# Hedgehog linear attention and a sigmoid GLU on one core: k tiles every six steps, a first h tile in a nest, q tasks, numerators and weight loads in other places

## The chip, the cores and the metric

One core of a Trainium2 chip. The metric is the device time of one execution in microseconds (us); given are the median, the lowest and the highest of three runs, and one further execution that was profiled. The engines are TensorE (PE, matmuls and transposes), VectorE (DVE), ScalarE (ACT), GpSimd (POOL) and SyncE (SP), which issues all the large transfers of this kernel in one queue, in order.

## The reference

x is 2048 rows (tokens) by 1024, all in fp32. It is normalised, then feeds two branches that are multiplied:

```python
def _A_ref(x, wqkv, w_phi, wo):           # H = 32 heads of 32
    q, k, v = split heads of x @ wqkv
    pq = jnp.einsum("bhsd,hdf->bhsf", q, w_phi)
    pk = jnp.einsum("bhsd,hdf->bhsf", k, w_phi)
    phi_q = jnp.concatenate([_softmax(pq, axis=-1), _softmax(-pq, axis=-1)], axis=-1)
    phi_k = jnp.concatenate([_softmax(pk, axis=-1), _softmax(-pk, axis=-1)], axis=-1)
    kv = jnp.einsum("bhsf,bhsd->bhfd", phi_k, v)
    z  = jnp.einsum("bhsf->bhf", phi_k)
    num = jnp.einsum("bhqf,bhfd->bhqd", phi_q, kv)
    den = jnp.einsum("bhqf,bhf->bhq", phi_q, z)[..., None] + 1e-6
    o = num / den
    return o (heads joined) @ wo

def _B_ref(x, w_gate, w_up, w_down):      # F = 3584
    g = jnp.einsum("bsd,df->bsf", x, w_gate)
    u = jnp.einsum("bsd,df->bsf", x, w_up)
    h = _sigmoid(g) * u
    return jnp.einsum("bsf,fd->bsd", h, w_down)

xn = _layernorm(x, axis=-1)
return x + _A_ref(xn, ...) * _silu(_B_ref(xn, ...))
```

## The kernel before

**Products.** An fp32 value is held as two reduced-precision parts: the rounded value (a cast on ACT, L135) and what is left (a subtraction on DVE, L136; "the low half" below). `mm3` (L144 to L146) is one fp32 product from three matmuls, high × high, high × low and low × high. The large products use a seven-product scheme: instead of eight products of quarter matrices there are seven, named B11, B21, T2, T3, T4, T1 and B22, of sums and differences of quarters. Weight sums are made by POOL and ACT (L483 to L485 for the GLU), stored or kept in SBUF, and then split into `w` tiles by `prep`, eight slots ahead at most.

**Stages.** First the projections of q, k and v, with the head transform `w_phi` folded into the weights of q and k, for one half of the rows, then the GLU's first pass; the projections for the other half; the second pass, pass 1 in the code (`begin_pass(1)`, L1476), which makes products T2, T3 and T4 for 14 tiles f of the hidden width; pass 2, which makes T1 and B22; then the down projection; and last an output loop over 8 pairs of row tiles, whose order is the list `PAIR`.

In pass 1 an f takes three groups of four banks. One bank is 12 matmuls, and after each comes a tick: so 12 ticks for an f, 168 for the pass. In the group T4 the gate of banks 0 and 1 is a sigmoid (L1429), banks 2 and 3 are multiplied onto it by DVE (`h_direct`, L1431), and ACT then copies the partial sum of the next f from memory into the bank (`seed`, L1392), so that T2 of the next f can accumulate there. PE waits for that copy.

In pass 2 most f are a `nest` (L1536): T1 and B22 of neighbouring tiles together, where the B22 product of a tile is itself made by seven smaller products, with its own operands (`x_nest_load`, `x_nest_sums`, `x_nest_split`). A nest has 90 matmuls and six ticks. In it ACT copies one partial result into the bank of the next product; L1612 is the copy from bank c to bank a, which product T4 accumulates onto. Before, pass 2 begins with plain T1 of tile 0, plain B22 of tile 0 and plain T1 of tile 1, and then come nests 1 to 12.

**Side work.** Everything that isn't the main product is queued by `later(n, f, ...)`: f is issued at the n-th tick from now. `k_steps` does one tile of 128 rows of k and v: load, maxima and minima per head (L663, L664), differences (L673, L674), one exponential (L677), sums and inverses (L682), scaling (L719), the low part (L727), and eight matmuls of the kv product (L735). Twelve of the 32 tiles are done during the projections, 20 in pass 1. `k_end` sums up a half of the heads. `q_steps` does the same features for a tile of q; four of these tasks run in pass 2, and they load from `qkv_d` at L951. `k_steps` tells the tiles of the projections from those of pass 1 by `wide`.

The order of instructions in one engine is set by this text order and by the scheduler of the framework, which moves instructions inside an engine by its own timeline; stretches marked `in_order` stay as they are written. An engine works its instructions strictly in order, so one that waits holds all those behind it.

Of the kernel before, what the change touches and what calls it, by code (L numbers as in the profile page):

```python
# [21 lines left out]
TT = S // P  # L22
# [27 lines left out]
def hedgehog_glu_kernel(  # L50
# [63 lines left out]
    LEAD = 2  # L114
    BEHIND = 'DVE', 'Activation', 'SP'
# [304 lines left out]
    ops += [("glu", 2, 0, T1), ("glu", 2, 0, B22), ("glu", 2, 1, T1)]  # L420
    ops += [("nest", 2, f, B22) for f in range(1, NJ - 1)] + [("glu", 2, NJ - 1, B22)]
# [17 lines left out]
    entry = {0: ops.index(("glu", 0, 0, B11)), 2: ops.index(("glu", 2, 1, T1))}  # L439
# [1021 lines left out]
    def begin_pass(p):  # L1461
# [14 lines left out]
        elif p == 1:  # L1476
            gates_r.items = halves(45, 46)
            gates_r.n = 0
            for n, f, *a in ((165, x_nest_load, 2, 0, 0), (166, x_nest_load, 2, 0, 1), (166, x_nest_load, 2, 1, 0),
                             (171, x_nest_load, 2, 1, 1), (170, x_nest_sums, 2, 0), (175, x_nest_sums, 2, 1),  # L1480
                             (176, x_nest_split, 2, T2), (177, x_nest_split, 2, T3), (179, x_nest_split, 2, T4)):
                later(n, f, *a)
            at = 1
            for t in range(EARLY, 2 * TT):
                k_steps(int(at), *divmod(t, TT))
                at += 7
                if t % TT == TT - 1:
                    k_end(int(at) + 8, t // TT)
                    at += 16
        else:  # L1490
# [3 lines left out]
            for n in range(4):  # L1494
                q_steps(13 + 18 * n, 6 + n // 2, n % 2)
# [3 lines left out]
    nest_raw = {0: ((43, 44), (54, 44)), 2: ((47, 50), (51, 53))}  # L1499
# [16 lines left out]
    def x_nest_split(p, i, hs=(0, 1)):  # L1516

        if i == T4:
# [7 lines left out]
        if i == T1 and p:  # L1526
            uvfree.extend(halves(47, 51))
# [110 lines left out]
    for n, (kind, c, what, i) in enumerate(ops):  # L1638
# [76 lines left out]
        if (phase, i) == (2, T1):  # L1715
            fetch_sum(2, f + 1)
            if f == 0:
                fetch_sum(1, 1)
# [41 lines left out]
        elif phase == 1 and f == NJ - 1:  # L1760
# [5 lines left out]
            else:  # L1766
                for b in (3, 5):
                    block(f"x{b}", 4 * b, 4, F32)
                uvfree.extend(halves(12, 13, 14, 15, 20, 21, 22, 23, 45, 46))
# [6 lines left out]
        elif (phase, f, i) == (2, 1, T1):  # L1776
# [111 lines left out]
    for k in range(4):  # L1888
        wo_prep(B22, k)
# [17 lines left out]
    for n in range(2):  # L1907
# [7 lines left out]
        gB110 mT4- xT4h- gB111 vB22- xT4l- gB112 mT1- tr100 gB113 hi100 lo100 tr001 gT20 hi001 aT1- lo001 tr000 gT21  # L1915
# [138 lines left out]
```

## Time and profile before

| what | us |
|---|---|
| median of three runs | 2344.85 |
| lowest, highest | 2343.36, 2347.31 |
| the profiled execution | 2340.34 |
| its span, first to last instruction | 2338.5 |
| PE busy | 2325.4 (99%) |
| DVE, ACT, POOL busy | 1687.9, 1252.6, 1120.4 |

The profile is of one execution. Times in its rows count from the start of its span. A row of the timeline reads: start, duration, engine, line, operation, output and inputs by name with shape and type, and in brackets how long the engine stood idle just before and what ended that; a matmul's duration there is from its issue to its end, and they overlap. A row of a group reads: line, engine, operation, count, then busy us, the mean of one in ns, and idle time ahead of it. The bound engine is PE, so the view of its waits is the one to begin with.

### The profile page before, as it was taken

To read this page: it belongs to the slowest core of one execution; us is meant where nothing else is said; L and a number is where in the kernel's file an instruction comes from. 1 tells how busy PE (TensorE), PEld (TensorE's weight loads), DVE (VectorE), ACT (ScalarE), POOL (GpSimd) and SP (SyncE) were. 2 spreads that over 40 slices of the span, in tenths; PEclk is the share of its full clock that TensorE was granted. 3 is DMA by queue.
4 is the path that set the end of the run, shared out by engine and by line. 5 is a ranking of instruction groups with operands and counts; after the bars stand their busy time and mean duration, and the time that the engine had idled before them with its cause. 6 is when DMAs were issued, how large, how long until landed. Compare 5 with 4: busy or idle time off the path is not lost.

```text
span 2338.5 us, 32642 instructions
## 1 busy us (share of the span) xinstructions
PE 2325.4 (99%) x10822; PEld 1939.5 (83%) x10822; DVE 1687.9 (72%) x2143; ACT 1252.6 (54%) x2000; POOL 1120.4 (48%) x797
## 2 busy tenths in 40 slices
PE   9999999999999999999999999999999999999999
PEld 8888888888888888888888888878888888888887
DVE  8624767776888765668656766674899878877786
ACT  7354577766555555555555555553444444355553
POOL 0323436781141055656541776674665444424566
PEclk9999999999999999999999999999999999999999
DMA  8799987988879777888795976779877667785665
GB/s 299 260 311 361 338 294 274 352 315 302 277 262 302 265 256 259 314 304 286 263 321 178 325 236 221 254 271 358 288 256 265 225 208 248 251 283 203 206 204 180
DMA packets 305018, 635.68 MB, mean 272 GB/s; under 512 B 38609, under 2 KB 38865, under 8 KB 300241
## 3 DMA queue, kind: packets, MB, share of 16 engines
q1 hardware_dynamic: 304848, 633.60, 78.5%
q8 instruction: 84, 1.38, 0.2%
q14 instruction: 86, 0.70, 0.1%
HBM read 380.50 MB, written 252.97 MB: 271 GB/s over the span
## 4 chain that ended last, share of the span: by engine, by line
PE 95%; DMA 1%; DVE 1%; ACT 1%; POOL 1%; issue 1%; SPq 0%; POOLq 0%; DVEq 0%; ACTq 0%
PE bank L144 30%; PE bank L146 30%; PE bank L145 30%; PE bank L1076 1%; PE bank L735 1%; PE bank L1052 1%; PE bank L379 1%; PE bank L1326 0%; DMA wf_d<-p 0%; PE bank L247 0%; DMA fc<-e_d 0%; DMA wd_d<-fb 0%; DMA fc<-qkv_d 0%; DMA fb<-w_gu 0%; DMA wd_d<-fa 0%
## 5 line engine op out<-in xcount | busy, mean ns | idle before, releaser
L144 PE MATMUL bank<-x,w 128*128 128x512 f32 x2252 | 877.1, 390 | 2.5 <-ACT bank L1392 2.2
L145 PE MATMUL bank<-x,w 128*128 128x512 f32 x2252 | 877.0, 389 | 0.0
L146 PE MATMUL bank<-x,w 128*128 128x512 f32 x2252 | 875.9, 389 | 0.0
L136 DVE TENSOR_TENSOR w<-fa,w 128x512 fp32r<-128x512 f32 (+2 forms) x388 | 378.4, 981 | 324.2 <-ACT w L135 315.8
L144 PEld LDWEIGHTS bank<-x,w 128*128 128x128 f32 x2252 | 423.1, 188 | 91.2 <-ACT bank L1392 3.1
L146 PEld LDWEIGHTS bank<-x,w 128*128 128x128 f32 x2252 | 422.9, 188 | 87.7
L145 PEld LDWEIGHTS bank<-x,w 128*128 128x128 f32 x2252 | 423.1, 188 | 87.1
L135 ACT CAST w<-fa 128x512 fp32r<-128x512 f32 (+2 forms) x388 | 265.1, 685 | 333.7 <-PE bank L145 233.9
L144 PE MATMUL bank<-w,x 128*128 128x512 f32 x708 | 277.5, 392 | 0.0
L146 PE MATMUL bank<-w,x 128*128 128x512 f32 x708 | 276.0, 390 | 0.0
L145 PE MATMUL bank<-w,x 128*128 128x512 f32 x708 | 276.0, 390 | 0.0
L136 DVE TENSOR_TENSOR w<-fb,w 128x512 fp32r<-128x512 f32 (+1 forms) x120 | 113.1, 947 | 67.6 <-ACT w L135 67.4
L146 PEld LDWEIGHTS bank<-w,x 128*128 128x128 f32 x708 | 133.0, 188 | 27.9 <-DVE x L1252 0.3
L144 PEld LDWEIGHTS bank<-w,x 128*128 128x128 f32 x708 | 133.0, 188 | 26.3 <-ACT bank L635 0.2
L145 PEld LDWEIGHTS bank<-w,x 128*128 128x128 f32 x708 | 133.1, 188 | 26.2
L135 ACT CAST w<-fb 128x512 fp32r<-128x512 f32 (+1 forms) x120 | 72.9, 609 | 115.4 <-PE bank L145 81.7
L136 DVE TENSOR_TENSOR x<-fb,x 128x512 fp32r<-128x512 f32 (+1 forms) x83 | 91.4, 1104 | 20.8 <-ACT x L135 19.8
L1396 ACT COPY fc<-bank 128x512 f32<-128x512 f32 x116 | 66.7, 584 | 42.5 <-PE bank L146 20.6
L136 DVE TENSOR_TENSOR p<-fc,p 128x512 fp32r<-128x512 f32 (+1 forms) x68 | 53.2, 793 | 33.3 <-ACT p L135 32.7
L1090 POOL TENSOR_TENSOR fc<-fc 128x512 f32<-128x512 f32 x32 | 48.9, 1527 | 59.2 <-DVE fc L1085 23.9
L135 ACT CAST x<-fb 128x512 fp32r<-128x512 f32 (+1 forms) x83 | 63.0, 761 | 10.9 <-DMA fb<-xo_d 5.6
L310 POOL TENSOR_TENSOR fb<-fb 128x512 f32<-128x512 f32 x6 | 9.9, 1648 | 112.9 <-DMA fb<-w_gu 76.1
(403 smaller groups left out, 3851.7 us busy)
## 6 DMA issues: line engine op xcount, KB each, us to landing
m_d<-fc SPq DMA_DIRECT2D x168, 256.0 KB, 4.2
fa<-h_d SPq DMA_DIRECT2D x147, 256.0 KB, 4.3
x<-m_d SPq DMA_DIRECT2D x130, 256.0 KB, 4.8
fa<-wf_d SPq DMA_DIRECT2D x32, 1024.0 KB, 6.6
fa<-w_gu SPq DMA_DIRECT2D x102, 256.0 KB, 5.0
h_d<-fc SPq DMA_DIRECT2D x96, 256.0 KB, 5.2
fc<-e_d SPq DMA_DIRECT2D x48, 512.0 KB, 5.8
fc<-qkv_d SPq DMA_DIRECT2D x88, 256.0 KB, 5.3
```

Of the source, the lines that this page charges most:

```text
L135: nc.scalar.copy(o[0], src)
L136: i = nc.vector.tensor_sub(o[1], src, o[0].bitcast(F32))
L144: nc.tensor.matmul(o, a[0], b[0], start=first, stop=False, **kw)
L145: nc.tensor.matmul(o, a[0], b[1], start=False, stop=False, **kw)
L146: last_mm[:] = [nc.tensor.matmul(o, a[1], b[0], start=False, stop=last, **kw).ins]
L310: nc.gpsimd.tensor_add(a22, a21, a22)
L379: nc.tensor.matmul(ps[:, gs], r[:, gs], bd[:, 4 * f + g], start=g == 0, stop=g == 3, skip_group_check=True)
L735: nc.tensor.matmul(kvb[g // 2][:, g % 2 * 256:g % 2 * 256 + 256], v[:, g].rearrange("p a f -> p (a f)"), ph[:, g].rearrange("p a f -> p (a ...
L1052: nc.tensor.transpose(ps[:, j * P:(j + 1) * P], e[:, k * P:(k + 1) * P], ident)
L1076: nc.tensor.matmul(ps[:, j * 256:(j + 1) * 256], kg[:, k], ph[:, a, k], start=a == 0, stop=a == 1)
L1090: nc.gpsimd.tensor_sub(o, a, b)
L1396: nc.scalar.copy(o, banks[b])
```

## The change

Four parts, in one edit:

1. In pass 1 a k tile starts every six ticks from tick 0 (`KAT`), where it was every seven from tick 1; its exponential, inverses, scaling and low part come one tick earlier than they did there. The x operands of pass 2's nests are loaded and split at ticks 152 to 169, where it was 165 to 179.
2. Pass 2 begins with plain T1 of tile 0 alone, and nests 0 to 12 follow.
3. The q tasks of pass 2 start at tick 7 (`CQ`) and every 18 from there, where it was 13, in a pass whose nests begin eight ticks earlier: so two ticks later in the nest that carries them. Those are the 2nd, 5th, 8th and 11th nest in both.
4. In `PAIR`, products (`gB..`, `gT..`) stand ahead of numerators (`nm...`), transposes and copies that they followed, and the preparation of weights B22 is written into the first pair (`w0` to `w3`), where it stood ahead of the loop.

```diff
+    KAT, CQ = 0, 7
...
-    ops += [("glu", 2, 0, T1), ("glu", 2, 0, B22), ("glu", 2, 1, T1)]
-    ops += [("nest", 2, f, B22) for f in range(1, NJ - 1)] + [("glu", 2, NJ - 1, B22)]
+    ops += [("glu", 2, 0, T1)] + [("nest", 2, f, B22) for f in range(NJ - 1)] + [("glu", 2, NJ - 1, B22)]
...
-    entry = {0: ops.index(("glu", 0, 0, B11)), 2: ops.index(("glu", 2, 1, T1))}
+    entry = {0: ops.index(("glu", 0, 0, B11)), 2: ops.index(("glu", 2, 0, T1))}
...
-        for n, f in ((0, k_load), (4, k_extremes), (5, k_spread), (7 + wide, lambda *a: exponentials(e_k)),
-                     (9 + wide, k_inverses), (10 + wide, k_scale), (11 + wide, k_low), (13 + 2 * wide + (t < TT - 1), kv_products)):
-            later(at + n, f, hb, t)
+        for n, f in ((0, k_load), (4, k_extremes), (5, k_spread), (7, lambda *a: exponentials(e_k)),
+                     (9, k_inverses), (10, k_scale), (11, k_low), (13 + (1 + wide) * (t < TT - 1), kv_products)):
+            later(max(at + n, 1), f, hb, t)
...
-            for n, f, *a in ((165, x_nest_load, 2, 0, 0), (166, x_nest_load, 2, 0, 1), (166, x_nest_load, 2, 1, 0),
-                             (171, x_nest_load, 2, 1, 1), (170, x_nest_sums, 2, 0), (175, x_nest_sums, 2, 1),
-                             (176, x_nest_split, 2, T2), (177, x_nest_split, 2, T3), (179, x_nest_split, 2, T4)):
+            for n, f, *a in ((152, x_nest_load, 2, 0, 0), (153, x_nest_load, 2, 0, 1), (154, x_nest_load, 2, 1, 0),
+                             (159, x_nest_load, 2, 1, 1), (158, x_nest_sums, 2, 0), (163, x_nest_sums, 2, 1),
+                             (164, x_nest_split, 2, T4, (0,)), (165, x_nest_split, 2, T4, (1,)), (166, x_nest_split, 2, T2), (169, x_nest_split, 2, T3)):
                 later(n, f, *a)
-            at = 1
+            at = KAT
             for t in range(EARLY, 2 * TT):
-                k_steps(int(at), *divmod(t, TT))
-                at += 7
+                k_steps(at, *divmod(t, TT))
+                at += 6
                 if t % TT == TT - 1:
-                    k_end(int(at) + 8, t // TT)
-                    at += 16
+                    k_end(at + 7, t // TT)
+                    at += 18
...
-                q_steps(13 + 18 * n, 6 + n // 2, n % 2)
+                q_steps(CQ + 18 * n, 6 + n // 2, n % 2)
...
-    for k in range(4):
-        wo_prep(B22, k)
...
-        hi000 e01 aT4- vB11 lo000 tr101 gT22 e11 hi101 lB22- nm001 lo101 lB21- nm000 cp001 yT1- gT23 yT4- cp000
-        ad001 gB210 ad000 nm011 vT2 gB211 cp011 ad011 tr010 gB212 hi010 lo010 gB213 mB22- tr110 nm010 hi110 aB22-
+        hi000 e01 aT4- vB11 lo000 gT22 tr101 e11 hi101 lB22- gT23 lo101 lB21- gB210 nm001 cp001 yT1- nm000 yT4- cp000
+        ad001 gB211 vT2 ad000 gB212 nm011 cp011 ad011 tr010 gB213 hi010 lo010 mB22- tr110 w0 w1 nm010 hi110 aB22- gT30
...
+        (r"w(\d)", False, lambda p, k: p or wo_prep(B22, int(k))),
```

Buffers follow (`nest_raw[2]`, the free halves of block 47 and 51, the fetch of a second partial sum that the first plain tiles needed). Most lines after the first added one stand one number higher in the changed kernel (L135 becomes L136), those near the end two lower (L1802 becomes L1800).

**The end of f = 9 in pass 1, on ACT.** T4 of f = 9 sets banks 0 to 3 (`bank_101` to `bank_104`) free for the seeds of f = 10; `w_94<-fa_97` is the cast of a later weight, `p` and `fc` belong to a k tile. Before:

```order
L1396 COPY fc_100<-bank_104 128x512
L1429 ACT_TABLE_LOAD
L1429 ACTIVATE fb_99<-bank_101 128x512
L1392 COPY bank_101<-x_3_6196 128x512
L135 CAST w_94<-fa_97 128x512
L1429 ACTIVATE fb_99<-bank_102 128x512
L1392 COPY bank_102<-x_3_6196 128x512
L135 CAST p_1_4483<-fc_100 128x8x64
L1392 COPY bank_103<-x_3_6196 128x512
L720 CAST p_4482<-fc_100 128x8x128
L135 CAST w_94<-fa_97 128x512
L1392 COPY bank_104<-x_3_6196 128x512
```

And in the changed kernel:

```order
L1429 ACTIVATE fb_99<-bank_102 128x512
L1392 COPY bank_102<-x_3_6196 128x512
L720 CAST p_4482<-fc_100 128x8x128
L1392 COPY bank_103<-x_3_6196 128x512
L1392 COPY bank_104<-x_3_6196 128x512
L136 CAST w_94<-fa_97 128x512
L1396 COPY fc_100<-bank_101 128x512
L677 ACT_TABLE_LOAD
```

The last seed, of `bank_104`, has moved from behind the weight's cast to ahead of it.

**The last nest with a q task, on DVE and ACT.** `fc_100` and `stq` belong to the q task, `w_94` are weights, `bank_105` and `bank_107` the nest's banks a and c. DVE before:

```order
L1437 TENSOR_TENSOR fc_100<-fc_100,bank_104 128x512
L136 TENSOR_TENSOR w_94<-fa_97,w_94 128x512
L663 TENSOR_REDUCE stq_11642<-fc_100 128x16
L664 TENSOR_REDUCE stq_11642<-fc_100 128x16
L1437 TENSOR_TENSOR fb_99<-fb_99,bank_101 128x512
L673 TENSOR_TENSOR fc_100<-fc_100,stq_11642 128x16x32
L674 TENSOR_TENSOR fc_100<-stq_11642,fc_100 128x16x32
L136 TENSOR_TENSOR w_94<-fa_97,w_94 128x512
L1570 TENSOR_TENSOR x_3_9768<-x_3_9768,bank_105 128x512
```

DVE in the changed kernel:

```order
L1437 TENSOR_TENSOR x_3_9819<-x_3_9819,bank_101 128x512
L137 TENSOR_TENSOR w_94<-fa_97,w_94 128x512
L663 TENSOR_REDUCE stq_11551<-fc_100 128x16
L664 TENSOR_REDUCE stq_11551<-fc_100 128x16
L1570 TENSOR_TENSOR x_3_9819<-x_3_9819,bank_105 128x512
L137 TENSOR_TENSOR w_94<-fa_97,w_94 128x512
L137 TENSOR_TENSOR w_94<-fa_97,w_94 128x256
L673 TENSOR_TENSOR fc_100<-fc_100,stq_11551 128x16x32
L674 TENSOR_TENSOR fc_100<-stq_11551,fc_100 128x16x32
```

The reductions now come after the add of the nest's first plain group, and the differences after the last two low halves. ACT before:

```order
L677 ACT_TABLE_LOAD
L677 ACTIVATE fc_100<-fc_100 128x1024
L1579 COPY p_2_10023<-bank_108 128x512
L135 CAST w_94<-fa_97 128x512
L1571 COPY bank_101<-bank_105 128x512
L1575 ACT_TABLE_LOAD
L1575 ACTIVATE x_3_9768<-x_3_9768 128x512
L135 CAST w_94<-fa_97 128x256
L1612 COPY bank_105<-bank_107 128x512
```

ACT in the changed kernel:

```order
L1579 COPY p_2_9738<-bank_108 128x512
L136 CAST w_94<-fa_97 128x512
L136 CAST w_94<-fa_97 128x256
L1571 COPY bank_101<-bank_105 128x512
L1575 ACTIVATE x_3_9819<-x_3_9819 128x512
L677 ACT_TABLE_LOAD
L677 ACTIVATE fc_100<-fc_100 128x1024
L1612 COPY bank_105<-bank_107 128x512
L1439 ACT_TABLE_LOAD
```

The exponential (L677) has moved from ahead of the nest's other work to directly ahead of L1612.

**The start of the output loop, on SP.** `g_d` takes results of the down projection, `e_d` and `wo_d` are loads for the loop. Before:

```order
L1802 DMA g_d<-x_5_12056 128x512 x2
L1904 DMA fc_100<-g_d 128x512
L1802 DMA g_d<-x_5_12056 128x512
L1042 DMA fc_100<-e_d 128x1024
L1802 DMA g_d<-x_5_12056 128x512
L1042 DMA fc_100<-e_d 128x1024
L1037 DMA x_6_16216<-wo_d 128x1024 x4
```

And in the changed kernel:

```order
L1800 DMA g_d<-x_5_12069 128x512 x2
L1900 DMA fc_100<-g_d 128x512
L1800 DMA g_d<-x_5_12069 128x512 x2
L1042 DMA fc_100<-e_d 128x1024 x2
L1037 DMA x_6_16229<-wo_d 128x1024 x4
```

Both stores now stand ahead of both `e_d` loads; the loads of `wo_d` follow as before.

More of the change, by code (lines that the diff above doesn't have):

```diff
@@ L1516, in x_nest_split @@
     def x_nest_split(p, i, hs=(0, 1)):
-        if i == T4:
+        if i == T4 and 0 in hs:
             block("p", 36, 2, F32R)
@@ L1526, in x_nest_split @@
         if i == T1 and p:
-            uvfree.extend(halves(47, 51))
+            uvfree.extend(halves(47))
             hs_r.items = halves(48, 49) + [slots[50][:, 0]]
@@ L1716, in hedgehog_glu_kernel @@
             fetch_sum(2, f + 1)
-            if f == 0:
-                fetch_sum(1, 1)
         finish()
@@ L1775, in hedgehog_glu_kernel @@
                 fetch_sum(1, 0)
-        elif (phase, f, i) == (2, 1, T1):
+        elif (phase, f, i) == (2, 0, T1):
             x_nest_split(2, T1)
```

10 lines of the change are left out of this document (5 added, 5 removed).

## The prediction

> **What bounds the kernel now.** The page first: the profiled execution took 2340.34 us, of which the span is 2338.5 us, so 1.84 us lie around it.
>
> ```profile
> span 2338.5 us, 32642 instructions
> PE 2325.4 (99%) x10822; PEld 1939.5 (83%) x10822; DVE 1687.9 (72%) x2143; ACT 1252.6 (54%) x2000; POOL 1120.4 (48%) x797
> ```
>
> TensorE (PE) is busy 99% of the span. Nothing can be won but matmuls left out or gaps between them. The view of waits (engine, line, what it waited for: total us, times, longest) lists the gaps:
>
> ```profile
> PE bank L144 <- ACT bank L1612: 2.7, 1, 2.7
> PE bank L144 <- ACT bank L1392: 2.2, 2, 1.7
> PE bank L1326 <- POOL ident masks.py:199: 1.5, 1, 1.5
> PE bank L1052 <- DMA fc<-e_d: 1.2, 1, 1.2
> ...
> PE bank L144 <- ACT bank L1600: 0.2, 1, 0.2
> ```
>
> About 8 us in all. 1.5 us of it is the start, which the change doesn't touch. So the change can win 2.7 + 2.2 + 1.2 + 0.2 = 6.3 us of gaps, what the clock lost behind them, and the removed matmuls. What it can lose is new gaps, because every other engine's work that it moves stands ahead of some copy that PE waits for.
>
> **(a) Six matmuls fewer.** The nests' side of the change replaces two plain products and one nest by other nests: an h tile of four plain groups and its partner are 2 × 48 matmuls, a nest 90, so one more nest is 96 − 90 = 6 fewer. A matmul's step comes from the chain: eight kv products end each stretch of 84 matmuls.
>
> ```profile
> 1020.60 0.95 PE bank L735 x8
> 1040.62 0.95 PE bank L735 x8
> ```
>
> (1040.62 − 1020.60 − 0.95) / 84 = 0.227 us; six are **−1.36 us**. They stand on the path with certainty, so no bounds are needed.
>
> **(b) k tiles every six ticks.** A tick is 12 matmuls, 2.72 us. Before, a k tile came every 7 ticks while an h tile takes 12, so the tile's work slid past the h tile's own side work, and twice it landed badly:
>
> ```profile
> 1157.42 0.62 ACT L135 CAST w<-fa 128x512 fp32r<-128x512 f32 x1 [4.65 <-POOL fa L484]
> 1157.95 0.58 ACT L1392 COPY bank<-x 128x512 f32<-128x512 f32 x1
> 1158.59 0.50 PE L144 MATMUL bank<-x,w 128*128 128x512 f32 x1 [0.57 <-ACT bank L1392]
> 1192.68 1.21 DVE L719 TENSOR_TENSOR fc<-fc,stk 128x1024 f32<-128x1024 f32 x1
> 1193.81 0.67 DVE L1431 TENSOR_TENSOR fb<-fb,bank 128x512 f32<-128x512 f32 x1
> 1194.52 0.59 ACT L1392 COPY bank<-x 128x512 f32<-128x512 f32 x1 [4.96 <-DVE fb L1431]
> 1195.16 0.50 PE L144 MATMUL bank<-x,w 128*128 128x512 f32 x1 [1.68 <-ACT bank L1392]
> ```
>
> In the first, the copy that seeds bank 3 (L1392) stands on ACT behind the cast of a later weight, and the cast waited 4.65 us for POOL's sum. In the second, the gate product on DVE (L1431), after which the bank may be seeded, stands behind the k tile's scaling (L719). Two tiles in twelve ticks fix the phase: every h tile gets the same two phases. In the new order the seed of bank 3 stands ahead of that cast at f 9 to 10 and 10 to 11, and the gate product ahead of the scaling at each h tile. So both gaps go: **−2.2 us**. The danger is the entry of f 9, where the new order has the seed behind such a cast:
>
> ```profile
> 1120.80 1.28 POOL L484 TENSOR_TENSOR fb<-fb 128x512 f32<-128x512 f32 x1
> 1124.24 0.39 PE L144 MATMUL bank<-x,w 128*128 128x512 f32 x1
> ```
>
> The sum ends 1122.08; cast 0.62 and seed 0.59 more: 1123.29, 0.95 us ahead of the matmul. I cost it at nothing; with POOL an operation of 1.28 us later it is 0.33 us. Bounds: −2.2 (none comes back) to −0.5 (one as long as the longest, 1.7, does). The 20 tiles end some 20 ticks earlier. Loads, sums and splits of the nests' x move with them from 165–179 to 152–169 of 168 ticks, and the first nest's fetches stand where the first h tile's stood. The last split, at 169, is 3 ticks or 8 us ahead of the first nest at 168 + 4; before, 179 was one tick ahead of 168 + 12. Cost nothing. Without that cover the first nest would wait for the copy of one split, some 0.6 us. The SP queue's loads move along with them and meet the same stores.
>
> **(c) q tasks two ticks later in each nest.** This decides the result. Four nests of pass 2 carry a q tile's features. The fourth lost most:
>
> ```profile
> 1531.46 0.43 SPq L951 DMA_DIRECT2D fc<-qkv_d  x1
> 1536.99 0.69 DVE L663 TENSOR_REDUCE stq<-fc 128x16 f32<-128x512 f32 x1 [5.61 <-DMA fc<-qkv_d]
> 1538.90 0.64 ACT L1439 ACTIVATE fb<-fb 128x512 f32<-128x512 f32 x1 [7.03 <-DVE fb L1437]
> 1546.56 0.58 ACT L1612 COPY bank<-bank 128x512 f32<-128x512 f32 x1
> 1547.19 0.50 PE L144 MATMUL bank<-p,w 128*128 128x512 f32 x1 [2.75 <-ACT bank L1612]
> 1548.12 0.63 PE L144 MATMUL bank<-p,w 128*128 128x512 f32 x1
> 1551.10 0.47 PE L145 MATMUL bank<-x,w 128*128 128x512 f32 x1
> ```
>
> The load was issued 2.6 us after the nest began; the reduction held DVE for 5.61 us, the gate behind it held ACT for 7.03, and the copy into the bank of product T4 (L1612) came 2.75 us late. Then seven steps took 2.98 us instead of 1.59; with the steps at both ends I put the half clock at 1.5. With the 0.2 of L1600 in the same nest: 4.5 us. The new order puts the reductions behind the first low half of the next weights, some 6 us later in the nest, which covers this load. Removed: **−4.5 us**. If the load slips by as much again, up to all of it stays.
>
> The Trainium skill ("TensorE: Matmul & The Clock Gate", Part 1: The HAM clock gate) says that the clock halves after an idle window of about 3.4 us. The trace disagrees, with seven slow steps behind 2.75 us. By the rule the gap would have cost 1.5 less, and the sum below were 1.5 higher.
>
> The price: EXP (L677) and its inputs L673 and L674 now stand directly ahead of L1612, where before they stood a third of a nest earlier. A nest without q task shows the room, and other rows the durations:
>
> ```profile
> 1457.55 0.82 DVE L136 TENSOR_TENSOR w<-fa,w 128x256 fp32r<-128x256 f32 x1 [0.88 <-ACT w L135]
> 1458.30 0.68 DVE L1437 TENSOR_TENSOR fb<-fb,bank 128x512 f32<-128x512 f32 x1
> 1459.55 0.58 ACT L1612 COPY bank<-bank 128x512 f32<-128x512 f32 x1
> 1461.87 0.39 PE L144 MATMUL bank<-p,w 128*128 128x512 f32 x1
> 1541.88 1.06 ACT L677 ACTIVATE fc<-fc 128x1024 f32<-128x1024 f32 x1
> 1472.19 0.68 DVE L673 TENSOR_TENSOR fc<-fc,stq 128x512 f32<-128x512 f32 x1
> 1472.80 0.68 DVE L674 TENSOR_TENSOR fc<-stq,fc 128x512 f32<-128x512 f32 x1
> 1349.68 1.81 DVE L673 TENSOR_TENSOR fc<-fc,stq 128x512 f32<-128x512 f32 x1
> 1351.41 1.77 DVE L674 TENSOR_TENSOR fc<-stq,fc 128x512 f32<-128x512 f32 x1
> L674 DVE TENSOR_TENSOR fc<-stq,fc 128x512 f32<-128x512 f32 x4 | 5.5, 1364 | 0.0
> L673 DVE TENSOR_TENSOR fc<-fc,stq 128x512 f32<-128x512 f32 x4 | 3.9, 965 | 0.0
> ```
>
> After the last low half, DVE is free at 1458.30. Fast, L673 starts there, L674 0.61 later and ends 1459.59; EXP ends 1460.65, L1612 1461.23: 0.64 us early, price 0. Slow (1.73 + 1.77), L674 ends 1461.80, EXP 1462.86, L1612 1463.44: 1.57 late. One of them slow, 0.45 late. The group's means, 0.965 and 1.364, lie 0.26 and 0.63 of the way from 0.68 to the slow ends. By these shares both are slow in 16%, one in 57% of the tasks: 0.16 × 1.57 + 0.57 × 0.45 = 0.5 us a task. Worst, two of the operations ahead on DVE are slow too, 1.1 each: 3.8 late, and the half clock behind it, 1.5: 5.3. Four tasks: **+2.0 us**, bounds 0 and 21. I take the value by the shares because these rows are of the same two instructions; they may not hold at the new place.
>
> The Trainium skill ("SBUF — State Buffer", Who interferes with whom) says that a DVE operation with two SBUF inputs and a GpSimd operation that reads SBUF shut each other out for a whole instruction. The 0.68 and 1.8 us of one instruction agree. By the rule a POOL that is busy at the new place makes the slow case usual; that is the second rival below.
>
> **(d) The output loop.** Placing products of a pair one ahead of the numerators moves matmuls against transposes, no work. Only at the start of the loop does it show:
>
> ```profile
> 2132.80 0.41 SPq L1042 DMA_DIRECT2D fc<-e_d  x1
> 2134.06 0.42 SPq L1042 DMA_DIRECT2D fc<-e_d  x1
> 2138.61 0.66 PE L1052 MATMUL bank<-ident,fc 128*128 128x128 f32 x4 [1.17 <-DMA fc<-e_d]
> ```
>
> The gap there is the wait for the second pair's load. On SP the first such load now stands behind a further store, where the second stood: 2134.06, 1.26 later. The transposes that wait stand one product (three matmuls, 0.69) later. Net **+0.6 us**; bounds −1.2 (the gap goes) and +1.3 (the whole delay shows). The weight preparation that is written into the loop (w0 to w3) issues its four loads at the same place on SP as before: this part moves nothing, and costs nothing. If its splits came later than their products, each would cost up to 1 us, but they are due seven products on.
>
> **Sum:** −1.36 − 2.2 − 4.5 + 2.0 + 0.6 = −5.5. Against the profiled execution: 2340.34 − 5.5 = 2334.8 us. The runs shown have a median of 2344.85, 4.5 more than the profiled one; the same difference gives **2339.4 us**. About 0.2%, 4.7 us, is what a measurement of this kernel can tell from no change.
>
> **Rivals.** *Dearer q tasks* (not told from no change): 1 to 3 us each, as where one low half ahead is slow too; −5.5 − 2.0 + 8 (2 each) = +0.5, 2345.4 us. For it: in the nest quoted the low half before the last waited 0.88 on its cast, so DVE has no reserve there. Against: in that nest the last low half took 0.82.
>
> *EXP ahead of T4's copy* (slower): one mechanism, the EXP in front of L1612 with POOL at work at that place. Each of the four nests then pays 5.3: −7.5 + 21.2 = +13.7, 2358.5 us. It decides slower from (4.7 + 7.5) / 4 = 3.05 us a task, that is when L674 ends some 2 us behind the time of the plain slow case. For it: 1.8 us rows exist, POOL sums stand in each of these nests. Against: all operations ahead must be slow together, four times.
>
> *A seed behind the cast at each h tile* (slower): the fixed phase is the wrong one. The mean of the two gaps, 1.1 us, at 11 entries is 12.1; without the −2.2 the sum is −3.3 + 12.1 = +8.8, 2353.7 us. Against: the order has the seed behind a cast at one entry.
>
> *The change doesn't do what it says in (c)*: the load's place on SP is as before, and if it lands later still, the old gap stays: −5.5 + 4.5 = −1.0, 2343.9 us.
>
> **How the numbers follow.** Forecast 0.54, its own range 2336 to 2342 (q price 0 to 1 us each, D by its bounds); it holds −7.5 to −3.5, of which I put 0.44 below −4.7 and 0.10 above. Even cheaper, with the gap in (d) gone as well (2336): 0.03. Dearer q tasks 0.14, gap stays 0.04: same. EXP rival 0.14, seed rival 0.11: slower. So faster 0.47, same 0.28, slower 0.25. The range is 2335 to 2353: it leaves out most of the EXP rival, and half of the seed rival.
>
> **What would show it.** Right: six matmuls fewer on PE, no wait for L1392 of over 0.3 us in pass 1, none for L1612 over 1.6, a wait at the start of the output loop near 1.7 us, PE clock at 1.00 through the nests. Wrong: waits for L1612 in the second, fifth, eighth and eleventh nest (EXP rival); waits for L1392 repeated every 32.6 us (seed rival); a gap in a place not named here, above all at the first nest or the loop's start; or the executions around the median differing from the profiled one by more than the sum.

## The result and the profile after

The changed kernel took 2350.44 us (median of 8 runs, 2348.69 to 2355.0), the kernel before 2344.85 (8 runs beside them, 2341.39 to 2347.31). The ratio is 1.0028, with a 95% interval of 1.0018 to 1.0039: slower by 5.6 us, which is little but more than chance explains, where the prediction had 5.5 us faster. The profiled execution took 2349.81 us.

The head of its page, and then what PE waited for longest (engine, line, what it waited for: total us, times, longest):

```profile
span 2348.0 us, 32662 instructions
...
PE 2328.9 (99%) x10816; PEld 1941.1 (83%) x10816; DVE 1691.8 (72%) x2147; ACT 1246.7 (53%) x2003; POOL 1114.6 (47%) x801
```

```profile
PE bank L145 <- ACT bank L1612: 7.0, 3, 2.4
PE bank L1052 <- DMA fc<-e_d: 2.8, 2, 2.0
PE bank L145 <- ACT fc L1396: 1.9, 1, 1.9
PE bank L1326 <- POOL ident masks.py:199: 1.5, 1, 1.5
PE bank L145 <- ACT bank L1392: 0.5, 1, 0.5
```

PE has six records fewer (10816 against 10822), as the change says. Of the gaps that it was to close, that for L1612 went from 2.7 to 7.0 us, and that for the `e_d` load from 1.2 to 2.8. The two for L1392 (2.2) are gone at their old places, the entries of f 10 and f 11; a new one of 0.5 stands at the entry of f 9, and a new one of 1.9 for L1396. L1396 is the copy that keeps the partial sum of a bank of T2 or T3 before the next product accumulates onto it; the prediction did not speak of it.

**Pass 2.** The second of the nests with a q task, the fifth in all, in the changed kernel's timeline on DVE, ACT, POOL and PE (start, duration, in brackets the idle time before and what ended it):

```profile
1399.58 1.50 DVE L137 TENSOR_TENSOR w<-fa,w 128x256 fp32r<-128x256 f32 x1
1401.01 1.78 DVE L673 TENSOR_TENSOR fc<-fc,stq 128x512 f32<-128x512 f32 x1
...
1403.42 1.06 ACT L677 ACTIVATE fc<-fc 128x1024 f32<-128x1024 f32 x1 [2.49 <-DVE fc L674]
1404.38 0.58 ACT L1612 COPY bank<-bank 128x512 f32<-128x512 f32 x1
...
1399.05 1.75 POOL L1413 TENSOR_TENSOR fc<-fc 128x512 f32<-128x512 f32 x1
...
1405.01 0.54 PE L145 MATMUL bank<-p,w 128*128 128x512 f32 x1 [2.34 <-ACT bank L1612]
```

The exponential (L677) waits 2.49 us for L674, and the copy that PE needs (L1612) waits behind it. On DVE the last low half took 1.50 us and L673 1.78 while POOL ran its sums of h tiles (L1411 to L1414; the third is shown) without a pause. The nest took 24.63 us from its first matmul to the next nest's, the eighth 24.45 and the eleventh 23.12, against 20.40 for one without a gap. The first nest with a q task, the second in all, took 20.58. POOL was hardly at work there; the busy time of PE, PEld, DVE, ACT and POOL, clock and DMA in five us of the second and of the fifth nest, and the differences of the second:

```profile
1335.20:1340.20 5.00, 5.00 (x23) 4.13 (x23) 4.66 (x9) 3.42 (x5) 1.29 (x1) 1.00 0.91 270
1396.60:1401.60 5.00, 5.00 (x23) 4.13 (x22) 5.00 (x7) 2.81 (x4) 4.92 (x4) 1.00 0.90 307
```

```profile
1337.98 0.68 DVE L673 TENSOR_TENSOR fc<-fc,stq 128x512 f32<-128x512 f32 x1
1338.58 0.68 DVE L674 TENSOR_TENSOR fc<-stq,fc 128x512 f32<-128x512 f32 x1
```

**Pass 1.** The same picture at the gap for L1396, in the changed kernel's timeline on ACT and DVE:

```profile
1091.71 0.62 ACT L136 CAST w<-fa 128x512 fp32r<-128x512 f32 x1 [5.57 <-POOL fa L484]
...
1093.53 1.77 DVE L673 TENSOR_TENSOR fc<-fc,stk 128x512 f32<-128x512 f32 x1
1095.22 1.77 DVE L674 TENSOR_TENSOR fc<-stk,fc 128x512 f32<-128x512 f32 x1
...
1097.07 1.28 ACT L677 ACT_TABLE_LOAD   x1 [3.73 <-DVE fc L674]
1098.37 1.06 ACT L677 ACTIVATE fc<-fc 128x1024 f32<-128x1024 f32 x1
1099.33 0.60 ACT L136 CAST w<-fb 128x512 fp32r<-128x512 f32 x1
1099.84 1.06 ACT L1396 COPY fc<-bank 128x512 f32<-128x512 f32 x2
```

Here it is the k tile's exponential that waits for slow differences on DVE, with its table load behind that wait, and the keep copy (L1396) stands behind both; PE waited 1.86 us for it. Slow differences alone don't make this gap. In the tile one f earlier they were as slow (1.77 and 1.78 us), and PE did not wait:

```profile
1054.23 0.62 ACT L136 CAST w<-fa 128x512 fp32r<-128x512 f32 x1 [5.02 <-POOL fa L484]
...
1056.04 1.77 DVE L673 TENSOR_TENSOR fc<-fc,stk 128x512 f32<-128x512 f32 x1
```

There the cast of a weight, whose low half stands on DVE ahead of the differences, began 2.95 us before the kv products of that f (1057.18); at the gap it began 0.07 before them (1091.78), because POOL's sum for that weight came later. At the gap the late weight and the slow differences come together.

### The profile page after: what moved, and what is told of

Same layout as the page of the kernel before. It is cut to its first block, busy times and chain, and to the rows that moved or that the text cites. A ratio compares the mean times of both kernels' runs of the same rounds, so it can differ in the third digit from the quotient of the medians.

```text
span 2348.0 us, 32662 instructions
## 1 busy us (share of the span) xinstructions
PE 2328.9 (99%) x10816; PEld 1941.1 (83%) x10816; DVE 1691.8 (72%) x2147; ACT 1246.7 (53%) x2003; POOL 1114.6 (47%) x801
## 5 line engine op out<-in xcount | busy, mean ns | idle before, releaser
L137 DVE TENSOR_TENSOR w<-fa,w 128x512 fp32r<-128x512 f32 (+2 forms) x394 | 390.2, 996 | 298.4 <-ACT w L136 288.3
L136 ACT CAST w<-fa 128x512 fp32r<-128x512 f32 (+2 forms) x394 | 268.8, 684 | 335.9 <-PE bank L146 221.3
L137 DVE TENSOR_TENSOR w<-fb,w 128x512 fp32r<-128x512 f32 (+1 forms) x116 | 106.4, 918 | 78.8 <-ACT w L136 78.6
L136 ACT CAST w<-fb 128x512 fp32r<-128x512 f32 (+1 forms) x116 | 70.2, 605 | 113.7 <-PE bank L146 90.3
L1396 ACT COPY fc<-bank 128x512 f32<-128x512 f32 x116 | 66.5, 584 | 40.6 <-PE bank L147 18.7
L136 ACT CAST x<-fb 128x512 fp32r<-128x512 f32 (+1 forms) x87 | 65.4, 754 | 12.7 <-DMA fb<-xr_d 5.5
L677 ACT ACTIVATE fc<-fc 128x1024 f32<-128x1024 f32 x36 | 38.2, 1061 | 48.8 <-DVE fc L674 48.6
```

The costliest lines, as they stand in the source:

```text
L136: nc.scalar.copy(o[0], src)
L137: i = nc.vector.tensor_sub(o[1], src, o[0].bitcast(F32))
L677: nc.scalar.activation(e, e, AF.Exp)
L1396: nc.scalar.copy(o, banks[b])
```

## The experiments

The theory after the first look: an exponential whose inputs are late stands in ACT's queue ahead of a copy that PE needs, and its inputs are late because DVE's operations with two inputs in SBUF are slow beside POOL's sums. The rivals: chance from run to run; the exponential by itself; DVE by itself; the other parts of the change (nest 0, the output loop). Ratios below are to the kernel before on the same chip, with 95% intervals.

**The same kernels again.** The changed kernel, unaltered:

> The changed kernel once more, unaltered. If its gaps are set by the order of instructions, as I think, the waits for L1612 come back in the nests with q tasks, 7.0 us in three of them in its first profile, within 1.5 us, and those for L1396 (1.9) and the e_d load (2.8) too; ratio to the kernel before 1.0028. If they are chance (the phase of transfers), they move to other places or change by half and more.

Ratio 1.0033 (1.0021 to 1.0045). The waits came back: 8.0 us for L1612 in the same three nests, 1.9 for L1396 at 1098 us, 1.7 for the `e_d` load. So the places are set by the order; the sizes are not fixed: single waits for L1612 moved by up to 1.1 us, that for the load fell by 1.1, and L1392 went from 0.5 to 1.1. The kernel before, unaltered:

> The kernel before once more, unaltered. If its gaps are set by order, the 1.7 us for L1392 in pass 1 and the 1.2 us for the e_d load come back; the 2.7 us for L1612 in the eleventh nest hung on a load that was 2.6 us later than in the nests before and may not. If the gap in the eleventh nest stays away, the changed kernel had less to win than the 4.5 us of the prediction.

In its pass 1 the waits for L1392 came back (2.5 us), and that for the load (1.0). The 2.7 us for L1612 did not: 0.3 us. But PE waited 2.2 us for L1592 and 1.1 for a low half in other nests instead, and over its nests it lost 5.8 us against 20.40 each, where the first profile had lost 5.6. The kernel before loses about that much in pass 2, at places that change from one profile to the other.

**What slows the exponential's inputs.** POOL's products and sums of pass 2 as memsets of the same tiles:

```diff
-            nc.gpsimd.tensor_mul(us[b - 2], us[b - 2], us[b])
+            nc.gpsimd.memset(us[b - 2], 0.0)
```

and so for the gating of nests and the four sums of h tiles.

> The changed kernel, with POOL's products and sums in pass 2 (the gating of h and the four sums of h tiles) left out: each is a memset of the same tile, which reads nothing. The order on DVE and ACT around the q tasks is that of the changed kernel. Theory: it is POOL's reading that makes L673, L674 and the low halves ahead of them slow; then they take 0.7 us each in all four nests with q tasks, the copy L1612 ends at 14.3 to 14.9 us of its nest as in the first of them, and the waits for L1612 are under 0.5 us in all (7 to 8 before). Rival: the exponential ahead of L1612 costs by itself, or the order of the queue does; then 4 us or more of the waits stay.

One run, so that the waits count here and not the time: 2342.29 us, beside a median of 2344.71 for the kernel before. PE's waits and DVE's groups of L673 and L674 in pass 2 of this kernel, and below them the same groups of the changed kernel:

```profile
PE bank L145 <- ACT bank L1612: 0.2, 1, 0.2
...
L674 DVE TENSOR_TENSOR fc<-stq,fc 128x512 f32<-128x512 f32 x4 | 4.4, 1092 | 0.0
...
L673 DVE TENSOR_TENSOR fc<-fc,stq 128x512 f32<-128x512 f32 x4 | 3.8, 957 | 0.0
```

```profile
L673 DVE TENSOR_TENSOR fc<-fc,stq 128x512 f32<-128x512 f32 x4 | 6.0, 1501 | 0.0
...
L674 DVE TENSOR_TENSOR fc<-stq,fc 128x512 f32<-128x512 f32 x4 | 3.8, 952 | 0.0
```

The wait for L1612 fell from 7.0 to 0.2 us with the exponential and L1612 in the same order. So the exponential ahead of the copy does not cost by itself; POOL's work beside DVE makes it late, as the first nest with a q task of the changed kernel showed without any edit. Not all four pairs ran at 0.7 us, as I had expected: five of the eight operations took 1.23 us, all of them where POOL was at sums of weights, which this edit left in. One of them:

```profile
1338.79 0.76 POOL L533 TENSOR_TENSOR fb<-fa 128x256 f32<-128x256 f32 x1 [0.84 <-DMA fa<-wg_d]
...
1338.86 1.23 DVE L673 TENSOR_TENSOR fc<-fc,stq 128x512 f32<-128x512 f32 x1
```

That agrees with the Trainium skill ("SBUF — State Buffer", Who interferes with whom): a DVE operation with two SBUF inputs and a POOL operation that reads SBUF exclude each other, one that only writes does not count. L533 reads, with 256 columns, and cost 0.55 us (1.23 − 0.68); the reading sums of 512 columns cost 1.1.

The same edit in pass 1 alone (the four sums of h tiles):

```diff
-        nc.gpsimd.tensor_sub(s3, a11, a21)
...
+        add, sub = [(lambda o, a, b: nc.gpsimd.memset(o, 0.0)) if phase == 1 else g for g in (nc.gpsimd.tensor_add, nc.gpsimd.tensor_sub)]; sub(s3, a11, a21)
...
```

> The changed kernel, with POOL's four sums of h tiles in pass 1 left out (a memset of the same tile each); the order on ACT and DVE is that of the changed kernel. The 1.9 us for L1396 near 1098 us: in the profile the low half, L673 and L674 ahead of that exponential took 1.2, 1.8 and 1.8 us beside these sums. Theory: the same as in pass 2, so they take 0.7 us each and the wait for L1396 goes (under 0.3 us). Rival: the wait is set by the weight's sum that came late (the cast ahead waited 5.6 us for it), and 1 us or more stays.

One run, 2343.68 us beside 2344.11. No wait for L1396 is left; L1392 keeps 0.3. DVE and ACT of this kernel at the place of pass 1 shown above:

```profile
1091.44 0.68 DVE L673 TENSOR_TENSOR fc<-fc,stk 128x512 f32<-128x512 f32 x1
1092.04 0.68 DVE L674 TENSOR_TENSOR fc<-stk,fc 128x512 f32<-128x512 f32 x1
...
1089.63 0.62 ACT L136 CAST w<-fa 128x512 fp32r<-128x512 f32 x1 [4.91 <-POOL fa L484]
```

1.77 + 1.77 became 0.68 + 0.68, and the 2.2 us saved cover the gap of 1.9. But the run does not rule out the rival, the late weight: the cast ahead still waited 4.91 us (5.57 in the changed kernel), yet it began 2.72 us before the kv products of its f (1092.35), where it was 0.07 before them. That is 2.65 us earlier and covers the gap as well. The tile at 1056 us shows that slow differences need the late weight to make the gap; that the late weight needs them too follows only from the 2.2 us, and no run shows it alone.

**Where the exponential stands.** In pass 2 one tick later, alone:

```diff
-        for n, f in ((0, load), (5, first), (6, lambda: spread(hold[2], *hold[:2])), (7, lambda: exponentials(hold[1])),
-                     (8, sums), (9, keep)):
+        offs = (0, 5, 6, 8, 9, 10) if t >= 6 else (0, 5, 6, 7, 8, 9)
+        for n, f in zip(offs, (load, first, lambda: spread(hold[2], *hold[:2]), lambda: exponentials(hold[1]), sums, keep)):
```

> The changed kernel, with the exponential of the four q tasks of pass 2 one tick later (and the sums and stores behind it too); the reductions and differences on DVE stay where they are. Theory: the loss in pass 2 is the exponential standing in ACT's queue directly ahead of the copy L1612 while it waits for L674. Then the waits for L1612 (7.0 us) and the half clock behind them (some 4 us) vanish, about 11 us: 2339 to 2340 us. Rival: DVE is the one that is late (its operations between the last low halves and the add), with or without the exponential; then at least half of the 7.0 us stays, at L1612 or at the copies and adds around it, and the time at 2345 or above.

Ratio 1.0062 (1.0047 to 1.0077), 7 us worse than the changed kernel. The time is one that the rival allowed, but its reason, a late DVE, is not what the profile shows, and neither theory had said that it would get worse. No wait for L1612 was left, but 9.2 us for L1592, the first copy of the next nest. ACT in this kernel:

```profile
1349.19 1.28 ACT L677 ACT_TABLE_LOAD   x1
1350.49 1.06 ACT L677 ACTIVATE fc<-fc 128x1024 f32<-128x1024 f32 x1
1351.57 1.28 ACT L1575 ACT_TABLE_LOAD   x1
1352.86 0.63 ACT L1575 ACTIVATE x<-x 128x512 f32<-128x512 f32 x1
```

Nothing waits here; the exponential and the two table loads around it are a block of 3.7 us (1349.19 to 1352.86). L1592 stands two places on, at 1353.92, and has less room than that. The exponential's price is thus of two kinds: at L1612 its inputs are late, a tick later it is the block itself. At tick 5, the old place in the nest:

```diff
-    KAT, CQ = 0, 7
+    KAT, CQ = 0, 5
```

> The changed kernel with the q tasks at tick 5, the place in their nests that they had before (the exponential a third of a nest ahead of L1612). Theory of the exponential: no wait for L1612 from it, 11 us less than the changed kernel, unless the fourth load is late again, as in the kernel before (2.75 us, and 5 with the clock); so 2339 to 2345 us. Rival (the loss in pass 2 comes from nest 0 and the other moves): at least half of the 11 us stays.

Ratio 0.9996 (0.9987 to 1.0006), 2341.39 us, where the changed kernel on that chip had 2349.18: 7.8 us less, and no wait for L1612. Its L673 and L674 are about as slow as in the kernel before (means 0.95 and 1.23 us; 0.97 and 1.36 there), but the copy has a third of a nest behind them. The old place's late load cost nothing in this profile.

**One part alone.** K tiles every six steps in the kernel before, with `k_steps` and the loop of the changed kernel and KAT = 0:

```diff
-            at = 1
+            at = 0
...
-                at += 7
+                at += 6
...
-                    k_end(int(at) + 8, t // TT)
-                    at += 16
+                    k_end(at + 7, t // TT)
+                    at += 18
```

> The kernel before with k tiles every six steps alone (and the earlier exponentials and kv products that go with it); the x loads of pass 2 stay late. Theory: the gaps of pass 1 move, they don't go: 1.9 us for L1396 near 1098 us with the half clock behind it, and 0.5 to 2 for L1392 some 32 us later, in place of 0.6 and 1.7: pass 1 is 1 to 2 us longer than before, the time 0.5 to 2 us above the kernel before. Rival (the prediction): pass 1 loses its gaps, 2.2 us less.

Ratio 1.0012 (1.0003 to 1.0021), 2.8 us more. PE waited 1.8 us for L1396 at 1098 us and 1.1 for L1392 some 31 us later, as in the changed kernel. Not all of the 2.8 us need be pass 1: in this profile the nests lose 8.8 us, with 3.4 for L1612 in the eleventh, where the load of the q tile came late again:

```profile
1541.62 0.69 DVE L663 TENSOR_REDUCE stq<-fc 128x16 f32<-128x512 f32 x1 [5.84 <-DMA fc<-qkv_d]
```

The q tasks two ticks later in the kernel before (13 becomes 15):

```diff
-                q_steps(13 + 18 * n, 6 + n // 2, n % 2)
+                q_steps(15 + 18 * n, 6 + n // 2, n % 2)
```

> The kernel before with the q tasks two ticks later alone (13 becomes 15); the same order on ACT and DVE in their nests as in the changed kernel. Theory: waits for L1612 of 5 to 8 us in three of the four nests, with the half clock 9 to 11 us, against 0 to 5 in the kernel before: 5 to 9 us above the kernel before, 2347 to 2351. Rival: the loss in pass 2 belongs to nest 0 or to the earlier side work; then the time stays within 2 us of the kernel before.

Ratio 1.0008 (0.9998 to 1.0018): less than I expected, at most 4.2 us. Its profile has 7.4 us of waits for L1612 in three nests, and its nests lose 12.3 us against 5.6 and 5.8 in the two profiles of the kernel before; but that execution, 2350.59 us, was the slowest of its ten, and nothing on record shows where the other nine lose less. The output loop and the last weight loads as before, in the changed kernel:

```diff
+    for k in range(4):
+        wo_prep(B22, k)
...
-        hi000 e01 aT4- vB11 lo000 gT22 tr101 e11 hi101 lB22- gT23 lo101 lB21- gB210 nm001 cp001 yT1- nm000 yT4- cp000
+        hi000 e01 aT4- vB11 lo000 tr101 gT22 e11 hi101 lB22- nm001 lo101 lB21- nm000 cp001 yT1- gT23 yT4- cp000
...
```

> The changed kernel with the output loop's order and the place of the last weight loads as before. Theory: the wait for the e_d load at the loop's start falls from 2.0 to about 1.2 us and the later one (0.8 us) goes, 1.5 to 2 us less than the changed kernel: about 2348.5. Rival: the wait is set by the loads' own time; then it stays at 2.0 or above, and the time at 2350.

Ratio 1.0023 (1.0013 to 1.0034), against 1.0033 for the changed kernel on that chip: 2.3 us less by the medians, with intervals that overlap. Its wait for the `e_d` load is 0.9 us. From the first transpose of the output loop (L1052) to the end of the span this kernel takes 254.0 us, the changed one 256.3.

**Putting together what gains.** Tick 5 and the old loop, with the k tiles and nest 0 of the change:

```diff
-    KAT, CQ = 0, 7
+    KAT, CQ = 0, 5
...
-        hi000 e01 aT4- vB11 lo000 gT22 tr101 e11 hi101 lB22- gT23 lo101 lB21- gB210 nm001 cp001 yT1- nm000 yT4- cp000
+        hi000 e01 aT4- vB11 lo000 tr101 gT22 e11 hi101 lB22- nm001 lo101 lB21- nm000 cp001 yT1- gT23 yT4- cp000
...
```

> The changed kernel with the q tasks at tick 5 and the output loop as before; k tiles every six steps and nest 0 stay. From the two runs apart, 8 and 2 us less than the changed kernel: about 5 below the changed kernel's gain over the kernel before, that is a ratio of 0.9985 to 0.9990 to the kernel before. Rival: the gains overlap, and the ratio is 0.9995 or above.

Ratio 0.9980 (0.9971 to 0.9989): faster than both kernels, 4.7 us less than the kernel before. What is left in it is pass 1: 1.8 us for L1396 and 1.9 for L1392. So the k tiles' place was moved (KAT = 2, with the x loads of pass 2 two ticks later as well):

```diff
-    KAT, CQ = 0, 5
+    KAT, CQ = 2, 5
...
-                later(n, f, *a)
+                later(n + 2, f, *a)
```

> The kernel of the run cq5pair with the k tiles and the x loads of pass 2 two ticks later (KAT = 2): the exponential then stands ahead of the last copy of T2 in each h tile. Theory: where an exponential with late inputs stands ahead of a copy that PE waits for decides, and two ticks away the wait of 1.9 for L1396 with its half clock goes or moves to a place with more room: 2 to 4 us less than cq5pair. Rival: another copy takes the wait, 1 us or more in pass 1 at a new place, and the time is that of cq5pair within 2 us.

Ratio 1.0022 (1.0012 to 1.0031), some 10 us worse than KAT = 0, where 2 to 4 less had been expected: 4.2 us of waits for L1396 at five places, 3.8 for L1392 at two, 1.4 for the kv products and 2.1 for L1592. And KAT = 4, with the x loads two ticks later:

> The same with KAT = 4 (x loads two ticks later): the exponential stands ahead of the last copy of T3 and ahead of the last seed. Theory: the last seed is the copy with the least room, so the waits for L1392 grow, 2 us or more in all, and the time is above that of KAT = 2. Rival: no difference between the places, within 2 us of KAT = 2.

Ratio 0.9960 (0.9946 to 0.9974), and no wait for L1392 or L1396 at all, against the expectation that the last seed would be the worst place. In this kernel the last load of x overwrites the sums of k features before they are stored, so a part of the attention's denominators comes of other data; the amount of work is the same. With the x work placed behind that store (lines against the changed kernel):

```diff
-            for n, f, *a in ((152, x_nest_load, 2, 0, 0), (153, x_nest_load, 2, 0, 1), (154, x_nest_load, 2, 1, 0),
-                             (159, x_nest_load, 2, 1, 1), (158, x_nest_sums, 2, 0), (163, x_nest_sums, 2, 1),
-                             (164, x_nest_split, 2, T4, (0,)), (165, x_nest_split, 2, T4, (1,)), (166, x_nest_split, 2, T2), (169, x_nest_split, 2, T3)):
+            for n, f, *a in ((155, x_nest_load, 2, 0, 0), (156, x_nest_load, 2, 0, 1), (157, x_nest_load, 2, 1, 0),
+                             (163, x_nest_load, 2, 1, 1), (161, x_nest_sums, 2, 0), (166, x_nest_sums, 2, 1),
+                             (166, x_nest_split, 2, T4, (0,)), (169, x_nest_split, 2, T2), (170, x_nest_split, 2, T3), (171, x_nest_split, 2, T4, (1,))):
```

> The kernel of cq5pair with KAT = 4, and the loads, sums and splits of pass 2's x placed behind the last use of the tiles that they overwrite (loads at ticks 155 to 163, splits at 166 to 171); in the run kat4 the last load came two ticks too soon. Theory: the place of the exponential among the copies decides, and at KAT = 4 no copy of pass 1 has it ahead of it with late inputs: no wait for L1392 or L1396 over 0.3 us in pass 1, and a time of 2334 to 2337, a ratio of 0.996 to 0.997 to the kernel before. Rival: the gaps stayed away in kat4 because the early load changed the end of the k work; then 1.5 to 4 us come back in pass 1, and the time is that of cq5pair (0.998).

Ratio 0.9972 (0.9960 to 0.9984), 2336.81 us beside 2344.80 for the kernel before. Its waits of PE:

```profile
PE bank L146 <- DVE x L137: 1.5, 1, 1.5
...
PE bank L1052 <- DMA fc<-e_d: 1.3, 1, 1.3
```

Pass 1 has none. The first line is the price of the later x loads: nest 0 waits 1.5 us for a split of x. With the q tasks one tick later:

```diff
-    KAT, CQ = 4, 5
+    KAT, CQ = 4, 6
```

> The same with the q tasks at tick 6, one later: the exponential stands behind the last cast of the weights and ahead of the copies L1571 and L1575. Theory: between the two places the price lies between: 0 to 3 us more than kat4b. Rival: it is the better place, since the load has another tick and L1592 waits less; then the time is 1 us or more below kat4b.

Ratio 0.9996 (0.9985 to 1.0006), 5.4 us more, beyond the 3 expected: 6.8 us of waits for L1612 in all four nests, though four operations now stand between. ACT of this kernel, from the exponential on:

```profile
1397.45 1.06 ACT L677 ACTIVATE fc<-fc 128x1024 f32<-128x1024 f32 x1 [0.63 <-DVE fc L674]
1398.42 0.58 ACT L1571 COPY bank<-bank 128x512 f32<-128x512 f32 x1
1399.02 1.28 ACT L1575 ACT_TABLE_LOAD   x1
```

The table that the exponential threw out has to come back for the gate (1.28 us), and that lies ahead of L1612 as well, which starts at 1401.72. Last, the changed kernel with KAT = 4 and that x work alone:

```diff
-    KAT, CQ = 0, 7
+    KAT, CQ = 4, 7
```

> The changed kernel with KAT = 4 and the x work placed as in kat4b; q tasks at tick 7 and the output loop as in the changed kernel. If the three losses are separate, pass 1 gives 3 to 4.5 us less than the changed kernel (1.9 for L1396, 0.5 to 1.1 for L1392, the half clock behind the first, about 1.6), and 7 us of waits for L1612 stay: a ratio of 1.001 to 1.002 to the kernel before. Rival: without the gaps in pass 1 the q tasks meet POOL otherwise, and half of the waits for L1612 or less stay.

Ratio 1.0013 (1.0003 to 1.0024): 7.6 us for L1612 stay, 0.3 for L1392, none for L1396. The two losses are separate.

## Why the prediction was wrong

It forecast 2339.4 us, from 2335 to 2353; 2350.44 lies inside the range, on the other side of the kernel before. Term by term:

| term | forecast, us | what the runs showed |
|---|---|---|
| (a) six matmuls fewer | −1.36 | six records fewer; no run of its own |
| (b) k tiles every six ticks | −2.2 | +2.8 alone (+0.7 to +4.9), perhaps not all of it in pass 1 |
| (c) old gap of pass 2 | −4.5 | the nests of the kernel before lose 5.6 and 5.8 in two profiles, at changing places; 8.8 in that of the k tiles alone |
| (c) price of the new place | +2.0 | 11.2 in the nests (4.23 + 4.05 + 2.72 + 0.18); 7.8 by the medians of ticks 7 and 5 |
| (d) output loop | +0.6 | +0.8 in the mean waits for `e_d`, +1.9 in the loop |

By medians the k tiles alone cost 2.8 us and the q tasks alone 2.4, and the old loop gave 2.3 back. With (a) that makes 6.1, beside 5.6 and 7.8 for the whole change in its two measurements.

**(c) is the step that failed most: the price of the new place.** The mechanism was seen: exponential, L673, L674 and POOL, with a worst case of 5.3 us a task and a break-even of 3.05. It cost 2.8 us a task in the profile. The price of 0.5 came of the sentence "By these shares both are slow in 16%, one in 57% of the tasks", with shares from the means at the old place, 5 us into the nest. At the new place POOL rests in only one of the four nests. The row was to be had from the kernel before, in a nest without q task, at the stretch that the operations were moved to (PE, PEld, DVE, ACT, POOL busy, clock, DMA):

```profile
1455.90:1460.90 5.00, 5.00 (x24) 4.14 (x23) 2.90 (x6) 2.53 (x5) 4.92 (x6) 1.00 0.11 40
```

POOL is busy 4.92 of 5 us there. And the operations ahead on DVE are slowed too: the last two low halves took 1.25 and 1.50 us in the nest shown, where they took 0.68 and 0.41 in the first nest with a q task. That is close to the case which the working kept for its worst: in the fifth and the eighth nest L673 was slow (1.78 and 1.77 us), L674 fast (0.68) and both low halves slow, in the eleventh all four. PE waited 2.34, 2.21 and 2.42 us for it. Most of the other 4.2 of the 11.2 us is the clock behind the first two waits, 1.7 us each, which the working adds only in its worst case. The prediction had the mechanism as two rivals, *dearer q tasks* and *EXP ahead of T4's copy*; the truth lay between their prices.

**The gain in (c)** was one execution's gap. Its place is set by the order, its size by how late a load is. In the eleventh nest the reduction waited 5.61 us for the load of the q tile in the first profile of the kernel before, 2.55 in the second and 5.84 in that of the k tiles alone, and PE waited 2.75, 0.32 and 3.38 us for L1612. In the second profile the kernel lost as much elsewhere in pass 2. And the move of the q tasks was not needed for the gain: in all five kernels with nest 0 and the q tasks at tick 5 no wait for L1612 is left.

**(b) failed at "So both gaps go".** The two gaps did go. But the danger that the prediction named and costed at nothing came, the seed behind a cast at the entry of f 9:

```profile
1130.87 0.62 ACT L136 CAST w<-fb 128x512 fp32r<-128x512 f32 x1 [5.63 <-POOL fb L484]
1131.40 0.58 ACT L1392 COPY bank<-x 128x512 f32<-128x512 f32 x1
```

PE waited 0.52 us there, 1.07 in the second profile of the same kernel, and up to 2.0 in other kernels with this phase. POOL's sum ended at 1130.84, 8.8 us later than in the row that the prediction used (1122.08), and the matmul was due only 7.3 us later (1131.52 against 1124.24); so the 0.95 us to spare became 0.5 too late. What else the new phase moves was not looked at: the exponential now stands ahead of a keep copy in T2 of every h tile (L1396), with inputs that POOL's sums slow, and where a weight comes late as well PE waits for the copy, 1.86 us and the clock behind it. That a fixed phase can be right or wrong as a whole was in the seed rival, and KAT = 4 and KAT = 2 show both: no wait, and seven.

**(d)** was right in mechanism and too small. The waits for `e_d` average 2.17 us over the seven profiles with the new loop (1.7 to 2.8) and 1.34 over the ten with the old one (0.9 to 1.9): 0.8 more, near the 0.6. But from its first transpose to the end of the span the loop takes 256.3 us in the mean with the new order (254.9 to 257.8) and 254.4 with the old (253.9 to 255.6): 1.9 more, above the bound of 1.3. In three of the seven, with waits of 2.0 to 2.4 us, the clock halved behind the wait, which the term left out. On SP both loads stand behind both stores:

```profile
2139.59 1.57 SPq L1800 DMA_DIRECT2D g_d<-x  x2
2141.25 0.89 SPq L1042 DMA_DIRECT2D fc<-e_d  x2
```

**(a)** and the early side work of nest 0 cost nothing that shows: no wait at the first nests in the changed kernel. That k tiles and nest 0 together gain once the exponentials stand elsewhere, cq5pair and kat4b show; how much is due to each was not measured.

## What to carry to other kernels

An instruction that is moved in an in-order queue is to be priced at its new place: what its inputs meet there (here POOL, busy 4.92 of 5 us), what stands right behind it, and the table loads that it brings, not its duration at the old place. When a periodic side task is put in a fixed phase, go through all copies that the bound engine waits for, not only those that stalled before, and try several phases: here they lay 0.5% apart. A gap in one profile is a gain only if a second profile of the same kernel has it at the same place and of the same size.

## What the runs showed of the hardware

PE's clock after a gap was a matter of chance between two values. The same gap at the same place, in the changed kernel and in its second profile:

```profile
1100.47 0.51 PE L145 MATMUL bank<-x,w 128*128 128x512 f32 x1 [1.86 <-ACT fc L1396]
...
1102.33 0.63 PE L145 MATMUL bank<-x,w 128*128 128x512 f32 x1
1102.76 0.63 PE L146 MATMUL bank<-x,w 128*128 128x512 f32 x1
```

```profile
1100.78 0.50 PE L145 MATMUL bank<-x,w 128*128 128x512 f32 x1 [1.86 <-ACT fc L1396]
...
1102.27 0.40 PE L145 MATMUL bank<-x,w 128*128 128x512 f32 x1
```

After the first, matmuls step at 0.43 us (1102.33 to 1102.76) for about 3.4 us, a loss of 1.76 us; after the second, none, a loss of 0.16. Over all seventeen profiles, summing the 40 steps behind each gap in matmuls of one size against 0.227 us: of 32 gaps of 1.75 to 3.4 us, 19 cost another 1.5 us or more and 13 less than 0.2; of 18 gaps of 0.9 to 1.7 us none did. The Trainium skill ("TensorE: Matmul & The Clock Gate", Part 1: The HAM clock gate) has the clock halve after an idle window of about 3.4 us that runs freely. The chance agrees with a free-running window; the length does not, since 1.84 us can be enough here. So a gap of 2 us had a price of 2 or of 3.7 us from one run to the next, which can be a part of the spread of some 5 us between runs of one kernel.
